# A third warm-up burst on TensorE, one store moved to ScalarE's DMA queue, and a changed place for one write and one transposing DMA

## The chip, the cores and the metric

The kernel runs on one core of a Trainium2 chip. The metric is device time in microseconds (us) for one execution. The profile is one execution of the same program; its own time is given beside its span, which runs from the first to the last instruction.

## The reference

Two independent branches start from the same normalised input, and their sum is added to the input. Sizes: 2048 tokens, width 640, hidden width 1728, all in bf16.

```python
xn = layernorm(q)                        # 2048 x 640
# branch A: long convolution over the 2048 tokens, per channel
k_shift = sum over t in 0..3 of k shifted by t tokens, times shift_k[:, t]
kv = k_shift * v
y  = irfft(rfft(kv, 4096) * rfft(ssm_k, 4096))[:2048] + kv * ssm_D
A  = xn * y
# branch B: gated feed-forward
h  = sigmoid(xn @ w_gate) * (xn @ w_up)  # 2048 x 1728
B  = h @ w_down                          # 2048 x 640
out = q + A + B
```

## The kernel before

**Tiling.** The 2048 tokens are 16 token tiles of 128 tokens (`NQ`), with the tokens on the partitions; `acc` (128 x 16 x 640) is loaded with the input, has both branches added to it and is stored from. Branch B works on four groups `tr` of four token tiles: the group is normalised (`xn`), transposed (`xnT`, width on partitions), multiplied with 14 blocks of gate and up weights (`rec_fc`, line 775; 5 matmuls of 128x512 each), passed through sigmoid (ScalarE) and multiplication (VectorE), and multiplied with `wd` (`rec_down`, line 791). Branch A is a Fourier transform in four matmul stages (lines 510, 530, 578, 610) in ten steps, written between the matmuls of branch B.

**Order.** Every piece of work is an operation with a number, given in the order in which the functions record it. The list `ORDER`, written out by hand, is the order in which the operations are issued; each engine and each DMA queue takes its own from the list in that order and goes through them strictly one after the other. `ON_DVE` names the operations that run on VectorE where both VectorE and ScalarE could do them. The keys that an operation lists as read and written (`r=`, `w=`) serve only to find out what has to stand before it in `ORDER`. The waits of the program on the chip come from the tiles that the instructions really touch.

**Queues.** Nearly all DMAs are issued by SyncE's queue, SP; four of the first loads are issued by ScalarE's. A wait of one DMA holds back everything behind it on its queue.

**The beginning.** TensorE first runs `warm`, matmuls of a zeroed tile with nothing useful in their result: 61 of 84 columns (`WARM`, operation 4). VectorE computes the statistics of token tiles 0, 1 and 2 (`rec_stat`, lines 640 and 642; `mv` is mean and variance). Tile 0's normalised rows are transposed on TensorE (operation 101, line 706, into `pst0_0`); then a second part of `warm`, 12 of 85 columns (operation 109), follows; ScalarE copies the transposed tile to `xnT` (operation 102), and the first real matmuls (operation 156, line 754) read that copy.

**Group 1, at 38 to 60 us.** Five DMAs on SP matter here. Operations 70, 71 and 73 are loads of the input for token tiles 8 to 15, each for a quarter of the partitions (32 partitions, 320 KB; line 367); the fourth quarter, 72, is issued long before. Operation 145 (line 693) writes the normalised group 1 to a scratch tensor `xnd` in DRAM. Operation 577 (line 700) reads it back as a transposing DMA into `xnT` for group 1. In the order before, SP issues 145, 73, 70, 71, 577, and behind them seven loads of the convolution's filter (line 456). The statistics of tiles 8 to 15 run on ScalarE: eight sums (`rec_stat_act`, line 647), each over all partitions of a tile and so behind all four loads. Seven of the eight stand in ScalarE's order ahead of the first sigmoid of group 1 (line 736). The matmuls of line 775 write to two PSUM slots (`g`); a gate slot is free again after its sigmoid.

**The end.** `store` writes the result: tiles 0 to 7, 8 to 13 and tile 14 each as four DMAs of 32 partitions (line 631), and tile 15 in three DMAs by column ranges 0 to 320, 320 to 560, 560 to 640 (line 627), all on SP in this order. Each waits for VectorE's last additions to its part of `acc` (lines 619 and 802).

Of the kernel before, what the change touches and what calls it, by code (L numbers as in the profile page):

```python
# [15 lines left out]
ACT = mybir.ActivationFunctionType  # L16
# [6 lines left out]
NQ = S // P  # L23
# [21 lines left out]
def _dft_tables():  # L45
# [32 lines left out]

ORDER = [
# [38 lines left out]
]  # L118
ON_DVE = [
    38, 50, 104, 108, 141, 142, 144, 148, 151, 153, 184, 186, 201, 224, 322, 415, 442, 449, 472, 486, 490, 508, 520, 811  # L120
]


# [94 lines left out]
def kernel(  # L218
# [74 lines left out]
    plan = _Plan(SLOTS, ("c", "xq"))  # L293
# [42 lines left out]
    def dma(fn, nd, run, q="SP", few=0.0, **kw):  # L336
        few = few or (1.4 if nd <= 64 and run > 1000 else 1.0)
        plan.op({q: (0.48 + nd / 8000.0, lambda: fn(nc.sync if q == "SP" else nc.scalar))},
                size=1.05 * few * nd * (10.6 + run / 23.8) / 16e3 + 0.03, nd=nd, **kw)
# [283 lines left out]
    def store(m0, m1, pri, d0=0, d1=DM):  # L623
        key = [("acc", m, x) for m in range(m0, m1) for x in range(4)] if d1 - d0 == DM else (
            [("fin", m, (d0 > 0) + (d0 > 320)) for m in range(m0, m1)] + [("cv", m) for m in range(m0, m1)])
        if m0 >= PRM["ML"]:
            dma(lambda e: e.dma_start(oq4[:, :, m0:m1, d0:d1], acc[:, m0:m1, d0:d1]), 128,
                2 * (d1 - d0) * (m1 - m0), few=3.0, r=key, w=[("out", m0, d0)], pri=pri)
            return
        for q in range(4):  # L630
            dma(lambda e, q=q: e.dma_start(oq4[q][:, m0:m1, d0:d1], acc[32 * q:32 * q + 32, m0:m1, d0:d1]), 32,
                2 * (d1 - d0) * (m1 - m0), r=key, w=[("out", m0, d0, q)], pri=pri)

    MEAN, VAR, RST, TMP, EPS = range(5)

    def rec_stat(m, pri):
        b = f"bs{m}"
        ak = [("acc", m, q) for q in range(4)]
        for s2 in range(2):
            dve(320, 1, lambda s2=s2: nc.vector.bn_stats(tl[b][:, 6 * s2:6 * s2 + 6], acc[:, m, s2 * 320:(s2 + 1) * 320]),  # L640
                r=ak, w=[(b, s2)], alloc=[(b, "bs")] if s2 == 0 else (), pri=pri)
        dve(8, 1, lambda: nc.vector.bn_aggr(st[:, 0:2, m], tl[b].rearrange("p (a c) -> p a c", a=2)),  # L642
            r=[(b, 0), (b, 1)], w=[("mv", m)], pri=pri)
# [95 lines left out]
                r=[pk(1), (sg,)], w=[(hk, fc)], pri=pri - 2000)  # L739

    MG, MD = 213.5, 135.0
    WARM = (61, 84)

    def rec_first(pri):
        every = [(fc, u) for fc in range(2) for u in range(2)]
# [62 lines left out]
    FIX = -1e6  # L808
# [9 lines left out]
    def warm(n, w=512):  # L818
        for _ in range(n):
            nc.tensor.matmul(tl["wps"][:, 0, 0:w], lhsT=tl["warm"][:, 0:P], rhs=tl["warm"][:, 0:w], start=True, stop=True)  # L820
    plan.op({"PE": (4.4, lambda: warm(*WARM))}, r=[("warm",)], w=[("wps", 0)], alloc=[("wps", "c")], pri=FIX)
    for m in range(2):
# [28 lines left out]
    rec_norm(0, FIX + 5, True)  # L851
    rec_tp(0, FIX, True)
    plan.op({"PE": (1.5, lambda: warm(12, 85))}, r=[("warm",), ("xn0", 0)], w=[("wps", 1)], pri=FIX + 0.5)
    for m0, m1, k in ((4, 8, "LS1"), (8, NQ, "LNS")):
        if m0 == 4:
            for m in range(m0, m1):
                rec_stat(m, PRM[k])
        else:
            rec_stat_act(m0, m1, PRM[k])
        rec_rsq(m0, m1, PRM[k], 1.0 if m0 == 4 else 1.0 / DM)  # L860
# [73 lines left out]
```

## Time and profile before

| | |
|---|---|
| median of 3 runs | 243.39 us (242.72, 243.39, 245.96) |
| profiled execution, own time | 242.79 us |
| profiled execution, span | 241.0 us |
| TensorE (PE) matmul busy | 230.3 us, 96% of the span |
| VectorE (DVE) busy | 198.7 us, 82% |
| ScalarE (ACT) busy | 152.2 us, 63% |
| bytes moved by DMA | 43.73 MB, 181 GB/s |

PE is TensorE's matmuls and PEld its weight loads. Rows of the timeline begin with the start and the length in us; a number in square brackets is the time for which the engine stood idle before the row, with what ended that. The suffix q (SPq, ACTq) is an engine's sequencer, which issues DMAs. In the tables by stretch, each engine's busy time is followed by the number of its instructions, then come the granted TensorE clock, the mean busy share of the 16 DMA engines, and GB/s.

### The profile page before, as it was taken

How to read it: one execution, taken by the hardware profiler on the slowest of the kernel's cores; microseconds unless marked ns; L12 is line 12 of the kernel's file. 1: busy time of each engine (PE TensorE's matmuls, PEld its weight loads, DVE VectorE, ACT ScalarE, POOL GpSimd, SP SyncE). 2: the span in 40 equal slices, each digit the busy share in tenths (PEclk: the TensorE clock that was granted, in tenths of full speed). 3: DMA queues.
4: the chain of work that ended last, by engine and by line, in shares of the span. 5: the costliest groups of instructions: out<-in, count | busy, mean ns of one | idle time of the engine just before them, and what ended most of it. 6: DMA issues, size and time to landing. Idle time of an engine off the chain costs nothing.

```text
span 241.0 us, 8367 instructions
## 1 busy us (share of the span) xinstructions
PE 230.3 (96%) x3707; PEld 142.0 (59%) x3739; DVE 198.7 (82%) x281; ACT 152.2 (63%) x213; POOL 0.7 (0%) x6
## 2 busy tenths in 40 slices
PE   7899999999999999999999999999999999999980
PEld 7755446774445556765655555777656645557670
DVE  3726884689799988999999998898978799779960
ACT  2732332086787997367998898979797742664210
POOL 1000000000000000000000000000000000000000
PEclk9999999999999999999999999999999999999998
DMA  5999999999978698994998893597361898510871
GB/s 153 314 233 311 219 291 182 236 152 147 219 177 151 102 186 214 176 280 76 157 199 201 203 213 104 113 287 175 116 177 40 214 244 280 158 61 3 215 235 46
DMA packets 92792, 43.73 MB, mean 181 GB/s; under 512 B 69780, under 2 KB 89172, under 8 KB 92500
## 3 DMA queue, kind: packets, MB, share of 16 engines
q1 hardware_dynamic: 92564, 43.04, 78.6%
q8 instruction: 29, 0.48, 0.9%
q10 hardware_dynamic: 192, 0.16, 0.2%
q14 instruction: 7, 0.06, 0.1%
HBM read 30.74 MB, written 5.24 MB: 149 GB/s over the span
## 4 chain that ended last, share of the span: by engine, by line
PE 92%; DMA 2%; issue 2%; DVE 1%; ACT 1%; DVEq 0%
PE g L775 47%; PE g L791 26%; PE c L530 9%; PE c L578 4%; PE c L510 3%; PE c L610 2%; DMA acc<-in_A_q_dram 2%; PE c L754 1%; DVE bs L640 1%; ACT st L658 0%; ACT VV L653 0%; DVE VV L684 0%; PE g L706 0%; DVE st L642 0%; DVE st L660 0%
## 5 line engine op out<-in xcount | busy, mean ns | idle before, releaser
L775 PE MATMUL g<-xnT,w 128*128 128x512 bf16 x356 | 86.5, 380 | 1.3 <-issue 0.2
L791 PE MATMUL g<-wd,hT 128*128 128x320 bf16 (+2 forms) x462 | 65.1, 295 | 0.1
L775 PEld LDWEIGHTS <-w 128*128 128x128 bf16 x380 | 35.2, 98 | 39.5 <-issue 0.6
L791 PEld LDWEIGHTS <-hT 128*128 128x128 bf16 x462 | 43.1, 98 | 16.9
L329 ACT CAST S<-c 128x1024 bf16<-128x1024 f32 (+2 forms) x41 | 39.8, 1001 | 9.5 <-PE c L530 5.3
L736 ACT ACTIVATE sig<-g 128x512 bf16<-128x512 f32 x44 | 26.4, 602 | 26.2 <-PE g L775 24.0
L738 DVE TENSOR_TENSOR hT<-sig,g 128x512 bf16<-128x512 bf16 x44 | 30.1, 685 | 15.6 <-PE g L775 14.0
L775 PE MATMUL g<-xnT,VV 128*128 128x512 bf16 x132 | 31.8, 379 | 0.5
L329 ACT CAST T<-c 128x1024 bf16<-128x1024 f32 (+1 forms) x21 | 20.7, 1010 | 9.8 <-PE c L510 6.4
L484 DVE TENSOR_TENSOR P<-kt,sT 128x2048 bf16<-128x2048 bf16 x20 | 24.2, 1220 | 0.2
L530 PEld LDWEIGHTS <-Mt 64*128 64x128 f16 x1280 | 19.8, 95 | 5.8 <-issue 5.0
L530 PE MATMUL c<-T,Mt 64*128 64x64 bf16 x1280 | 22.1, 190 | 0.5 <-issue 0.5
L775 PEld LDWEIGHTS <-VV 128*128 128x128 bf16 x140 | 13.3, 98 | 15.0
L802 DVE TENSOR_TENSOR acc<-g,acc 128x320 bf16<-128x320 f32 (+2 forms) x33 | 15.7, 479 | 7.3 <-PE g L791 6.9
L329 ACT CAST VV<-c 128x1024 bf16<-128x1024 f32 x17 | 17.0, 1020 | 4.9 <-PE c L578 4.7
L332 ACT ACTIVATE T<-c 128x1024 bf16<-128x1024 f32 x18 | 18.1, 1026 | 1.3 <-PE c L510 1.3
L647 ACT ACTIVATE VV<-acc 128x640 bf16<-128x640 bf16 x9 | 6.6, 736 | 10.8 <-DMA acc<-in_A_q_dram 10.6
L562 DVE TENSOR_TENSOR S<-S 64x2048 bf16<-64x2048 bf16 x10 | 12.2, 1220 | 0.3
L559 DVE TENSOR_TENSOR S<-S 128x2048 bf16<-128x2048 bf16 x10 | 12.2, 1224 | 0.3
L564 DVE TENSOR_TENSOR S<-P 64x2048 bf16<-64x2048 bf16 x10 | 12.2, 1223 | 0.3
L488 DVE TENSOR_TENSOR P<-P,P 128x2048 bf16<-128x2048 bf16 x10 | 12.2, 1223 | 0.2
L552 DVE TENSOR_TENSOR P<-S,P 128x2048 bf16<-128x2048 bf16 x10 | 12.2, 1220 | 0.1
(75 smaller groups left out, 181.9 us busy)
## 6 DMA issues: line engine op xcount, KB each, us to landing
P<-S SPq DMA_DIRECT2D x20, 256.0 KB, 3.9
w<-in_B_w_up_dram SPq DMA_DIRECT2D x7, 640.0 KB, 6.4
w<-in_B_w_gate_dram SPq DMA_DIRECT2D x7, 640.0 KB, 6.7
kt<-in_A_k_dram SPq DMA_DIRECT2D x8, 320.0 KB, 7.3
xnd<-VV SPq DMA_DIRECT2D x4, 640.0 KB, 5.2
vt<-in_A_v_dram SPq DMA_DIRECT2D x8, 320.0 KB, 6.8
VV<-in_A_ssm_k_dram SPq DMA_DIRECT2D x16, 96.0 KB, 4.1
wd<-in_B_w_down_dram SPq DMA_DIRECT2D x3, 480.0 KB, 8.3
```

The costliest lines, as they stand in the source:

```text
L329: fa = lambda: nc.scalar.copy(out=out_fn(), in_=in_fn())
L332: fa = lambda: nc.scalar.activation(out_fn(), in_fn(), ACT.Copy, scale=scale)
L484: dve(2048, 2, lambda: nc.vector.tensor_tensor(tl[c].rearrange("p i (n c) -> p i n c", c=CJ), two(t), sh(t), ALU.mult), r=kr + [("s",)], w ...
L488: dve(2048, 2, lambda: nc.vector.tensor_tensor(tl[a][:], tl[a][:], tl[b][:], ALU.add), r=[(b,)], w=[(a,)], pri=pri)
L530: nc.tensor.matmul(tl[c][:, b, 64 * kk:64 * kk + 64], lhsT=Mb[rows, (k + 16 * b) % 32, 64 - 64 * r:192 - 64 * r], rhs=tl[T][rows, 2 * k + ...
L552: dve(n, 2, lambda: nc.vector.tensor_tensor(Q(), X(), Q(), ALU.mult), r=[(Z, "h", 0), (Z, "h", 1)], w=[(Z, 0)], pri=pri)
L559: dve(n, 2, lambda: nc.vector.tensor_tensor(X(), X(), H(), ALU.mult), r=[(Z, 0)] + sr, w=[(S_, "p")], pri=pri + 0.01)
L736: act(512, lambda: nc.scalar.activation(tl[sg][:], pv(0), ACT.Sigmoid), r=[pk(0)], w=[(sg,)], alloc=[(sg, "sig")], pri=pri - 2000)
L738: dve(512, 1, lambda: nc.vector.tensor_tensor(hT[:, fc, :], tl[sg][:], pv(1), ALU.mult), r=[pk(1), (sg,)], w=[(hk, fc)], pri=pri - 2000)
L775: nc.tensor.matmul(tl[c][:], lhsT=w()[:, k, o:o + P], rhs=tl[X][:, k, :], start=(k == 0), stop=(k == NC - 1))
L791: nc.tensor.matmul(tl[pd[i]][:, 0:d1 - d0], lhsT=hT[:, fc, t4 * P:(t4 + 1) * P], rhs=wd[:, fc, d0:d1], start=(fc == 0), stop=(fc == NFC - 1))
L802: dve(d1 - d0, 1, lambda i=i, m=m, pd=pd, d0=d0, d1=d1: nc.vector.tensor_tensor(acc[:, m, d0:d1], tl[pd[i]][:, 0:d1 - d0], acc[:, m, d0:d1 ...
```

## The change

Three things are changed in the code, and `ORDER` and `ON_DVE` follow.

- `WARM` is 57 matmuls of 90 columns instead of 61 of 84.
- A third part of `warm`, four matmuls of 256 columns, is recorded as a new operation 110. It lists tile 1's statistics (`mv`, 1) and tile 0's transposed rows as read. It stands in `ORDER` behind operation 102 and ahead of the first real matmuls.
- In `store`, the four DMAs of tile 14 are issued by ScalarE's queue instead of SP's. Their places in `ORDER` stay.

All operations from 110 on get a number one higher, and so do the entries of `ON_DVE`. With the numbers mapped, `ORDER` differs in one more place: operation 145 (now 146, the write to `xnd`) and 577 (now 578, the transposing DMA). SP's order was 145, 73, 70, 71, 577; it is 73, 70, 146, 578, 71.

```diff
@@ ORDER
-    86, 87, 88, 15, 102, 156, 103, 104, 531, 157, 46, 47, 48, 49, 532, 68, 66, 91, 67, 92, 69, 567, 16, 158, 569, 89,
+    86, 87, 88, 15, 102, 110, 157, 103, 104, 532, 158, 46, 47, 48, 49, 533, 68, 66, 91, 67, 92, 69, 568, 16, 159, 570,
...
-    523, 524, 525, 526, 556, 590, 143, 558, 596, 142, 591, 144, 145, 594, 597, 73, 600, 598, 599, 601, 37, 38, 178,
-    586, 70, 587, 71, 577, 589, 28, 31, 30, 29, 27, 25, 26, 39, 128, 177, 124, 127, 123, 130, 129, 580, 581, 179, 578,
...
+    558, 524, 525, 526, 527, 557, 591, 144, 559, 597, 143, 592, 145, 595, 598, 73, 601, 599, 600, 602, 37, 38, 179,
+    587, 70, 146, 578, 588, 71, 590, 28, 31, 30, 29, 27, 25, 26, 39, 129, 178, 125, 128, 124, 131, 130, 581, 582, 180,
...
@@ store
         for q in range(4):
             dma(lambda e, q=q: e.dma_start(oq4[q][:, m0:m1, d0:d1], acc[32 * q:32 * q + 32, m0:m1, d0:d1]), 32,
-                2 * (d1 - d0) * (m1 - m0), r=key, w=[("out", m0, d0, q)], pri=pri)
+                2 * (d1 - d0) * (m1 - m0), q="ACT" if m0 == NQ - 2 else "SP", r=key, w=[("out", m0, d0, q)], pri=pri)
...
-    WARM = (61, 84)
+    WARM = (57, 90)
...
     plan.op({"PE": (1.5, lambda: warm(12, 85))}, r=[("warm",), ("xn0", 0)], w=[("wps", 1)], pri=FIX + 0.5)
+    plan.op({"PE": (0.43, lambda: warm(4, 256))}, r=[("warm",), ("mv", 1), ("pst0_0", 0)], w=[("wps", 2)], pri=FIX + 0.5)
```

More of the change, by code (lines that the diff above doesn't have):

```diff
@@ L80 @@
     5, 1, 6, 8, 7, 10, 9, 13, 11, 12, 20, 0, 76, 77, 78, 79, 17, 19, 80, 96, 81, 82, 83, 18, 84, 4, 85, 97, 101, 109,
[37 rows of a table removed]
[37 rows of a table added]
 ]
 ON_DVE = [
-    38, 50, 104, 108, 141, 142, 144, 148, 151, 153, 184, 186, 201, 224, 322, 415, 442, 449, 472, 486, 490, 508, 520, 811
+    38, 50, 104, 108, 142, 143, 145, 149, 152, 154, 185, 187, 202, 225, 323, 416, 443, 450, 473, 487, 491, 509, 521, 812
 ]
```

68 rows, old and new, of the table ORDER are left out of this document.

## The prediction

> **What bounds the kernel now.** First the page: the span, the slices, and the chain of work that ended last.
>
> ```profile
> span 241.0 us, 8367 instructions
> ...
> PE   7899999999999999999999999999999999999980
> ...
> PEclk9999999999999999999999999999999999999998
> ...
> PE 92%; DMA 2%; issue 2%; DVE 1%; ACT 1%; DVEq 0%
> ```
>
> TensorE is busy from the second slice to the last but one, and 92% of the chain is its work. So time that TensorE stands still anywhere in the middle stays in the total; only the first 8 us and what follows the last matmul are bounded by others. The profiled execution took 242.79 us, 1.79 outside its span; the median of the three runs, 243.39, is 0.6 above it. I sum on 242.79.
>
> The change touches three places. I read the timeline at each.
>
> **The beginning.**
>
> ```profile
> 1.22 4.45 PE L820 MATMUL c<-sig 128*128 128x84 bf16 x61 [1.22 <-DVE sig L809]
> ...
> 6.12 1.03 PE L820 MATMUL c<-sig 128*128 128x85 bf16 x12
> ...
> 6.65 0.21 DVE L642 BATCH_NORM_AGGREGATE st<-bs 128x2 f32<-128x12 f32 x1
> ...
> 7.82 0.72 PE L754 MATMUL c<-xnT,VV 128*128 128x128 bf16 x10 [0.66 <-ACT xnT L329]
> ...
> 8.82 1.30 PE L754 MATMUL c<-xnT,VV 128*128 128x128 bf16 x20
> ```
>
> The clock shows in the spacing (the page's clock row shows 9 from the start and doesn't tell these). From 12 to 61 warm-up matmuls the time grows by 3.42 us, 70 ns for each 84 columns: 0.83 ns a column. From 10 to 20 matmuls of line 754 it grows by 0.58 us, 58 ns for 128 columns: 0.45. So the clock went from half to full between 7.15 and 7.82, in the 0.66 us in which TensorE waits for ScalarE's copy.
>
> 57 x 90 is 5130 columns against 61 x 84 = 5124: the same time. The new part is 1024 columns: 0.46 us at the fast spacing, 0.85 at the slow one. It fits into the 0.66 us or ends 0.19 after them (7.15 + 0.85 = 8.00). The wait for tile 1's statistics costs nothing: they are ready at 6.65 + 0.21 = 6.86, before the second part has ended; and as the new matmuls touch neither statistics nor transposed rows, I expect no such wait in the queue at all. Queued behind it are the matmuls of line 754, which wait for the copy anyway. I take **0**, with ends -0.2 and +0.2.
>
> [...]
>
> **The middle.** This part is not in the title of the change; it is in the order list, and I think that it decides.
>
> ```profile
> 32.95 5.51 SPq L432 DMA_DIRECT2D kt<-in_A_k_dram  x2
> 40.28 0.40 SPq L693 DMA_DIRECT2D xnd<-VV  x1
> 40.72 2.10 SPq L367 DMA_DIRECT2D acc<-in_A_q_dram  x3
> 43.89 4.86 SPq L700 DMA_TRANSPOSE xnT<-xnd  x1
> 48.79 4.93 SPq L456 DMA_DIRECT2D VV<-in_A_ssm_k_dram  x7
> ```
>
> SP's order of time. From 38.5 to 40.28 SP stands before the write (its waits name VectorE's normalisation):
>
> ```profile
> SPq L693 <- DVE VV L684: 1.8, 1, 1.8
> ```
>
> The change fills that pause with two of the three loads, and puts the third behind the transposing DMA. Who waits for the third load is in ScalarE's timeline, and who waits for ScalarE in TensorE's:
>
> ```profile
> 48.62 0.74 ACT L647 ACTIVATE VV<-acc 128x640 bf16<-128x640 bf16 x1 [10.56 <-DMA acc<-in_A_q_dram]
> ...
> 54.43 0.19 ACT L647 ACTIVATION_READ_ACCUMULATOR VV<-acc 128x1 f32 x1
> 55.21 0.60 ACT L736 ACTIVATE sig<-g 128x512 bf16<-128x512 f32 x1 [0.59 <-PE g L775]
> ```
>
> ```profile
> 44.42 9.67 PE L791 MATMUL g<-wd,hT 128*128 128x320 bf16 x70
> 53.93 1.24 PE L775 MATMUL g<-xnT,VV 128*128 128x512 bf16 x4
> 55.01 3.40 PE L775 MATMUL g<-xnT,w 128*128 128x512 bf16 x15
> ```
>
> ScalarE waits 10.56 us for the last of the loads, to 48.62; seven sums take it to 54.62, and its first sigmoid of group 1 at 55.21 waited only 0.59 us for TensorE. TensorE has two PSUM slots; its second group of five runs from 55.01 to about 56.09 (3.40 us less one length of 0.38 over 14 gaps is 0.216 a matmul), and the third needs the slot which the sigmoid frees at 55.81. So a load later by more than 0.59 + 0.28, about 0.8 us, stops TensorE for the excess.
>
> How late is it? In time on the DMA engines:
>
> ```profile
> 38.50:39.50 1.00, 1.00 (x9) 0.66 (x7) 0.69 (x2) 0.00 (x0) 0.00 (x0) 1.00 0.43 40
> ...
> 40.28:43.81 3.53, 3.53 (x28) 2.54 (x27) 0.98 (x2) 0.00 (x0) 0.00 (x0) 1.00 1.13 309
> 43.81:48.60 4.79, 4.79 (x37) 3.49 (x36) 4.01 (x6) 0.00 (x0) 0.00 (x0) 1.00 1.01 189
> ```
>
> The DMA share (last but one) is full from 40.28 on. The write lands 3.5 us after its issue (the least of line 693), and the transposing DMA lands 9.1 after its own (the least of line 700):
>
> ```profile
> DMA to landing us min/median/max: 3.5/5.2/6.5
> ```
>
> ```profile
> DMA to landing us min/median/max: 9.1/9.3/9.5
> ```
>
> So: write landed 43.8; three loads landed 48.6, 4.8 us later, 1.6 each; transposing DMA landed 43.89 + 9.1 = 53.0, 4.4 after the loads, 0.9 ahead of the matmuls that read it at 53.93.
>
> After the change, step by step:
> 1. Two loads are in the queue ahead of the write: its landing moves by 2 x 1.6 to **47.0** (46.0 if the hole at 38.5 takes some of them; 43.8 if all).
> 2. SP waits there; the transposing DMA is issued at 47.1. Another one in the trace blocked SP for 2.79 us:
>
> ```profile
> 97.31 2.79 SPq L700 DMA_TRANSPOSE xnT<-xnd  x1
> ```
>
> SP is free at 49.9. The third load is issued by 50.4.
> 3. With nothing ahead of it the transposing DMA lands between 47.1 + 4.4 = 51.5 and 47.1 + 9.1 = 56.2. In before, 4.7 of the 9.1 went by beside the loads, so the nearer row is the 4.4; with half a microsecond to start, 52.0. TensorE needs it at 53.93: no stall.
> 4. The third load is behind it in the same queue. At 1.0 us after, it lands at **53.0**, 4.4 later than 48.6. Less the 0.8 of slack, TensorE stops for **3.6 us** at about 56 to 60. Bounds: 0 (write not delayed: 43.89 + 2.79, then an issue and a short landing, about 49.4) and +7.8 (transposing DMA at 56.2, load at 57.2).
>
> The seven filter loads move back by 1.6 us (48.79 to 50.4). Their first use on TensorE is here, and moves by 3.6, which hides it:
>
> ```profile
> 60.50 0.41 PE L510 MATMUL c<-Ft,VV 32*128 32x64 f16 x32
> ```
>
> **The end.**
>
> ```profile
> 232.75 0.82 DVE L619 TENSOR_TENSOR acc<-acc,vt 128x1280 bf16<-128x1280 bf16 x1
> 233.67 0.49 DVE L802 TENSOR_TENSOR acc<-g,acc 128x320 bf16<-128x320 f32 x1
> 234.87 0.74 DVE L802 TENSOR_TENSOR acc<-g,acc 128x240 bf16<-128x240 f32 x2 [0.71 <-PE g L791]
> ```
>
> ```profile
> 233.60 1.71 SPq L631 DMA_DIRECT2D out_dram<-acc  x4
> 235.40 1.95 SPq L627 DMA_DIRECT2D out_dram<-acc  x3
> ```
>
> ```profile
> SPq L929 <- DMA out_dram<-acc: 2.1, 1, 2.1
> ```
>
> Tile 14's four issues hold SP until 235.31. Tile 15's first part was ready at 234.16, its last at 234.87 + 0.74 = 235.61. The three issues take 1.95 us, 0.65 each, the last from 236.7; then 2.1 us of landing. With the four on the other queue: first part 234.2 to 234.85, second (ready about 235.25) to 235.9, third to 236.55 instead of 237.35. ScalarE is idle there (its last row is a 0.69 us copy at 230.52) and has issued loads beside SP at no higher price:
>
> ```profile
> 0.73 1.84 ACTq L367 DMA_DIRECT2D acc<-in_A_q_dram  x4
> ```
>
> I take **-0.9**; nothing (0) if the stores share what limits the landing, -1.2 if the first part's start sets it.
>
> **Sum:** 242.79 + 0 + 3.6 - 0.9 = **245.5**.
>
> **The rivals.**
> *The load is not late (not slower).* If the two early loads go through in the hole of 38.5 to 39.5 (share 0.43) and in the 1.8 us for which SP stood, the write lands near 43.8, the third load near 49.4, and the middle costs nothing: 242.79 - 0.9 = 241.9. It decides where the third load lands before 49.4. For it: the pause is real. Against it: the two loads of `k` ahead on SP (32.95 + 5.51) end their issue only at 38.46, so data of theirs are still to come, and the share is 1.13 right after. Chance 0.2.
>
> *The clock falls in the new pause.* TensorE would stand for over 3 us. At the end of the kernel the clock record holds after the last matmul and has fallen later:
>
> ```profile
> 235.40:238.90 3.50, 0.00 (x0) 0.00 (x0) 0.21 (x1) 0.00 (x0) 0.00 (x0) 1.00 0.26 67
> 238.90:241.00 2.10, 0.00 (x0) 0.00 (x0) 0.00 (x0) 0.00 (x0) 0.00 (x0) 0.55 0.02 4
> ```
>
> So 3.5 us idle did not lower it, a little more did. If it falls, TensorE runs at half speed until it is raised; at the beginning that took at most 7.82 - 1.22 = 6.6 us, so up to 3.3 us are lost: 245.5 + about 3 = 248.5. Chance 0.1. [...]
>
> *The transposing DMA is slow on an empty queue too.* Landing toward 56.2 and the load behind it: 247.5 to 249.7. Chance 0.1.
>
> *The change doesn't do what it says:* no wait for the statistics exists in the queue. The time is the same 245.5, so it has no share of its own.
>
> **How the numbers follow.** Forecast 0.6 (243.5 to 247.0: write landing 46 to 47.5, load 0.5 to 1.6 behind the transposing DMA, end -0.4 to -1.2). The range goes from the first rival, 241.9, to the beginning of the two slow ones, 248.4. A measurement tells 2% from no change, 4.9 us here: 238.5 and 248.3. Nothing gives the former, 0.02; about two thirds of the slow rivals pass the latter, 0.14; the rest, 0.84, is within.
>
> **What would show it.** The new burst between 7.0 and 7.9 with line 754 still at about 7.8. SP's row of line 700 near 47 instead of 43.89, and a single load of line 367 behind it. ScalarE's line 647 starting near 53 instead of 48.62, idle for it about 15 us, and an idle gap of 3 to 4 us on TensorE before a group of line 775 at 59 to 60, with the sigmoid's row no longer waiting for TensorE. At the end, four stores on ACTq and the row of line 627 beginning at 234.2. I am wrong if line 647 starts before 49.5, if the pause is made up later, or if the granted clock dips behind it.

## The result and the profile after

The changed kernel took **251.6 us** (median of 6 runs, 249.5 to 252.8) against 243.61 us for the kernel before beside it (6 runs, 242.72 to 245.96): a ratio of 1.0309, 95% interval 1.0266 to 1.0353. It is 3% slower. The forecast was 245.5 us with a range of 241.9 to 248.4; the time lies outside it.

The profiled execution took 251.6 us, with a span of 249.8 against 241.0: 8.8 us to explain. First the page of the changed kernel: the span, the slices, the clock and the chain that ended last.

```profile
span 249.8 us, 8367 instructions
...
PE   8889999992999999999999999999999999999990
...
PEclk9999999998699999999999999999999999999998
...
PE 68%; DMA 13%; SPq 8%; ACT 6%; issue 2%; DVE 1%; DVEq 0%; ACTq 0%
```

Two things are new. In the tenth slice TensorE is busy for two tenths, and in the tenth and eleventh the granted clock is 0.8 and 0.6. The chain, 92% TensorE before, now goes for a quarter through DMA, SP and ScalarE. The number of instructions is the same. Apart from the third slice (8, before 9), the rest of these rows looks like before, so most of the loss should lie around 56 to 68 us.

**The middle.** SP's order of time, and its longest wait there:

```profile
40.32 1.89 SPq L367 DMA_DIRECT2D acc<-in_A_q_dram  x2
42.33 0.40 SPq L693 DMA_DIRECT2D xnd<-VV  x1
48.43 2.76 SPq L700 DMA_TRANSPOSE xnT<-xnd  x1
51.25 0.56 SPq L367 DMA_DIRECT2D acc<-in_A_q_dram  x1
51.87 4.20 SPq L456 DMA_DIRECT2D VV<-in_A_ssm_k_dram  x7
```

```profile
SPq L700 <- DMA xnd<-VV: 5.6, 1, 5.6
```

SP stands 5.6 us before the transposing DMA, until the write to `xnd` has landed; the third load comes behind. Then ScalarE and TensorE:

```profile
55.48 0.74 ACT L647 ACTIVATE VV<-acc 128x640 bf16<-128x640 bf16 x1 [16.63 <-DMA VV<-in_A_ssm_k_dram]
...
61.37 1.06 ACT L736 ACTIVATE sig<-g 128x512 bf16<-128x512 f32 x2
```

```profile
55.27 1.24 PE L775 MATMUL g<-xnT,VV 128*128 128x512 bf16 x4
56.35 1.24 PE L775 MATMUL g<-xnT,w 128*128 128x512 bf16 x5
62.00 4.42 PE L775 MATMUL g<-xnT,w 128*128 128x512 bf16 x10 [4.41 <-ACT sig L736]
```

ScalarE's first sum starts at 55.48 instead of 48.62, after 16.63 us of waiting for a DMA. (The row names a load of the filter: the releaser is inferred, and the sum reads `acc`, and nothing that the filter's load writes. By the trace's record of its semaphore, the third load landed at 55.45.) Seven sums later the two sigmoids run back to back at 61.37, no longer waiting for TensorE. TensorE stood for 4.41 us, up to 62.00.

Then a second loss: ten matmuls of 512 columns take 4.42 us, where the same ten took 2.32 elsewhere in this trace. The table by stretch shows the granted clock (the column behind POOL):

```profile
57.60:60.25 2.65, 0.00 (x0) 0.00 (x0) 0.63 (x1) 2.56 (x7) 0.00 (x0) 1.00 0.90 150
...
60.30:61.95 1.65, 0.00 (x0) 0.00 (x0) 0.00 (x0) 1.62 (x6) 0.00 (x0) 0.50 1.39 175
62.00:67.05 5.05, 5.05 (x12) 1.72 (x12) 2.56 (x4) 1.95 (x6) 0.00 (x0) 0.50 1.40 184
67.15:69.00 1.85, 1.85 (x20) 0.72 (x21) 1.05 (x2) 0.72 (x2) 0.00 (x0) 1.00 0.57 236
```

The clock fell 2.7 us into the pause and was at half until 67.1. TensorE worked through 5.1 us of that at half speed, and so lost about 2.5.

**The beginning.**

```profile
1.22 4.45 PE L820 MATMUL c<-sig 128*128 128x90 bf16 x57 [1.22 <-DVE sig L809]
...
5.99 1.06 PE L820 MATMUL c<-sig 128*128 128x85 bf16 x16
7.85 0.72 PE L754 MATMUL c<-xnT,VV 128*128 128x128 bf16 x10 [0.81 <-ACT xnT L329]
```

The third part of the warm-up follows the second at once; the row counts both, 12 and 4. Its 2044 columns took 1.06 us, the 1020 of before 1.03: in this execution the clock was already up. Nothing waits for tile 1's statistics. Line 754 starts at 7.85, against 7.82 before.

**The end.** The stores, and SP's wait ahead of line 627:

```profile
241.99 2.24 ACTq L631 DMA_DIRECT2D out_dram<-acc  x4
...
244.72 1.95 SPq L627 DMA_DIRECT2D out_dram<-acc  x3
```

```profile
SPq L627 <- DMA out_dram<-acc: 2.9, 1, 2.9
```

In the kernel before, the same wait was:

```profile
SPq L627 <- DVE acc L802: 0.3, 1, 0.3
```

Tile 14's stores are on ScalarE's queue, yet SP's row of line 627 doesn't begin earlier against the work that it follows, but later: 0.99 us behind the last matmul's end, which was 0.07 before. SP waited there 0.3 us for VectorE; now it waits 2.9 for a DMA that stores. The span ends 6.10 us behind the last matmul instead of 5.67.

**Together:** 4.4 (stop) + 2.5 (half clock) + 0.4 (end) = 7.3 of the 8.8 us. Another 1.3 is there before the middle begins (the first group of line 775 starts at 55.27 instead of 53.93), where TensorE waits for loads of weights:

```profile
PE g L775 <- DMA VV<-in_B_w_up_dram: 0.6, 1, 0.6
PE g L791 <- DMA wd<-in_B_w_down_dram: 0.4, 1, 0.4
```

The next experiments show the same groups at 54.23 to 55.07 in kernels with SP's order of before, so I don't count this part as the change's.

### The profile page after: what moved, and what is told of

The parts are those of the page before. It is cut to its first block, busy times and chain, and to the rows that moved or that the text cites. A ratio compares the mean times of both kernels' runs of the same rounds, so it can differ in the third digit from the quotient of the medians.

```text
span 249.8 us, 8367 instructions
## 1 busy us (share of the span) xinstructions
PE 233.3 (93%) x3707; PEld 142.4 (57%) x3739; DVE 198.7 (80%) x281; ACT 151.9 (61%) x213; POOL 0.7 (0%) x6
## 4 chain that ended last, share of the span: by engine, by line
PE 68%; DMA 13%; SPq 8%; ACT 6%; issue 2%; DVE 1%; DVEq 0%; ACTq 0%
PE g L775 32%; PE g L791 21%; PE c L530 7%; DMA acc<-in_A_q_dram 4%; PE c L578 4%; DMA wd<-in_B_w_down_dram 3%; SPq L367 3%; PE c L510 3%; SPq L421 2%; DMA P<-S 2%; PE c L610 2%; ACT VV L647 2%; DMA VV<-in_B_w_gate_dram 2%; DMA VV<-in_A_ssm_k_dram 1%; ACT VV L653 1%
## 5 line engine op out<-in xcount | busy, mean ns | idle before, releaser
L775 PE MATMUL g<-xnT,w 128*128 128x512 bf16 x356 | 88.8, 386 | 5.7 <-ACT sig L736 4.4
L775 PEld LDWEIGHTS <-w 128*128 128x128 bf16 x380 | 35.7, 99 | 45.3 <-issue 7.2
L775 PE MATMUL g<-xnT,VV 128*128 128x512 bf16 x132 | 32.4, 383 | 1.1 <-DMA VV<-in_B_w_up_dram 0.6
L775 PEld LDWEIGHTS <-VV 128*128 128x128 bf16 x140 | 13.4, 99 | 16.5 <-issue 1.1
L329 ACT CAST VV<-c 128x1024 bf16<-128x1024 f32 x17 | 17.0, 1020 | 4.9 <-PE c L578 4.7
```

Source lines behind the costliest of these rows:

```text
L329: fa = lambda: nc.scalar.copy(out=out_fn(), in_=in_fn())
L775: nc.tensor.matmul(tl[c][:], lhsT=w()[:, k, o:o + P], rhs=tl[X][:, k, :], start=(k == 0), stop=(k == NC - 1))
```

## The experiments

My theory after the traces: the changed place of 145 and 577 on SP makes almost all of the loss, by two steps, a stop behind the late third load and a clock that falls in the stop; the end costs a little, because tile 15's stores wait for tile 14's. The rivals: warm-up or stores take part in it; the late write and the late transposing DMA cost the time wherever the third load stands; the clock falls for a reason other than the pause; the two queues' stores slow each other.

A list of `ORDER` of another length moves the line numbers by two in e1, e2 and e4 (L777 for L775), and added lines move them by four to six in e8 to e13. "Behind the last matmul" is counted from the end of TensorE's last row.

### One part at a time: e1 to e4

e1 is the kernel before with only the changed order on SP:

```diff
-    ..., 144, 145, 594, 597, 73, ..., 586, 70, 587, 71, 577, 589, 28, ...
+    ..., 144, 594, 597, 73, ..., 586, 70, 145, 577, 587, 71, 589, 28, ...
```

> The kernel before with one thing changed: SP's order 73, 70, 145, 577, 71. Theory A (the late load is the loss): TensorE stops 4.6 us ahead of line 775 near 60 us, the clock falls to half for 5 to 7 us, and nothing else is lost: 243.6 + 4.6 + 2.5 = 250.7, 249.5 to 251.5. Rival B (the order costs only the stop of 3.6 that I predicted, the rest comes from the warm-up or the end): 247. Rival C (the loss of 1.3 us between 16 and 40 us in the changed kernel's profile also belongs to the order): 252.

e2 is the changed kernel with the order put back, e3 has only the four stores of tile 14 on ScalarE's queue, e4 only the warm-up (`WARM`, the third part, and its place).

> The changed kernel with SP's order put back to 145, 73, 70, 71, 577. Theory A: line 647 starts near 48.6 again, no stop and no fall of the clock; what is left is the end: 243.6 to 244.6. Rival B: 246 to 248. My prediction's term for the end: 242.7.

> The kernel before with tile 14's four stores on ScalarE's queue, nothing else. Theory D (the three stores of tile 15 wait for semaphores that the four stores of tile 14 have just taken): the row of line 627 begins about 2.7 us after the first of the four, at 236.3 instead of 235.40, and the time is 0.4 to 0.9 longer: 244.1 to 244.5. Prediction: the row begins at 234.2 and 0.9 is saved, 242.7.

> The kernel before with the warm-up in three parts, stores and order as before. Theory and prediction: no change, 243.4 to 243.8, the first matmuls of line 754 still at 7.8. Rival E (the 1.3 us lost between 16 and 40 us come from the beginning): 244.9, with TensorE waiting for a weight load near 16 us in the profile.

| | median us | ratio to before (243.13), 95% interval |
|---|---|---|
| e1, order alone | 250.1 (246.4 to 251.2, 4 runs) | 1.0221 (1.0146 to 1.0295) |
| e2, all but the order | 243.87 | 1.0012 (0.9984 to 1.0040) |
| e3, stores alone | 243.43 | 1.0025 (0.9996 to 1.0054) |
| e4, warm-up alone | 243.74 | 1.0024 (0.9999 to 1.0050) |

e1's ratio is worked out from its executions of 246.4 and 249.9 us alone; its median is 1.029 times that of the kernel before. The clearer comparison is the changed kernel (1.0309) with e2 (1.0012), which differ in nothing but the order; in e2 the sums begin at 49.79, and TensorE doesn't stop there. So the order alone makes the loss, and the two edits that give the change its name make none that 2% would show. e1's timeline of TensorE and its clock by stretch:

```profile
62.29 4.42 PE L777 MATMUL g<-xnT,w 128*128 128x512 bf16 x10 [4.98 <-ACT sig L738]
```

```profile
62.30:67.60 5.30, 5.30 (x13) 1.86 (x13) 2.55 (x4) 2.20 (x6) 0.00 (x0) 0.50 1.28 244
```

Stop and half clock are both there. One of e1's four executions, the one of 246.4 us, kept its clock (mean 0.997, the others 0.985 to 0.989); the others took 3.5 to 4.8 us more. How long TensorE stopped in it isn't known, as it was not profiled. All six executions of the changed kernel have means of 0.981 to 0.989.

e4's profile has the beginning of the changed kernel (line 754, here L756, at 7.72 behind a gap of 0.59) and an end like before. In e3 SP's stores of tile 15 begin 0.97 us behind the last matmul, with the same kind of wait as in the changed kernel:

```profile
237.70 1.95 SPq L627 DMA_DIRECT2D out_dram<-acc  x3
```

```profile
SPq L627 <- DMA out_dram<-acc: 3.5, 1, 3.5
```

e3's span ends 6.09 us behind the last matmul, as late as the changed kernel's. e3 and e4 also had short stops of about 1 us at 57 to 58, behind sums that began at 51.50 and 50.98; the order of before leaves the loads that little room, and its stop comes and goes with the execution.

### The place of the third load: e5

```diff
-    ..., 144, 145, 594, 597, 73, ..., 586, 70, 587, 71, 577, 589, 28, ...
+    ..., 144, 594, 597, 73, ..., 586, 70, 587, 71, 145, 577, 589, 28, ...
```

> The kernel before with all three input loads ahead of the write on SP: 73, 70, 71, 145, 577. It separates the place of the third load from the later write. Theory (the third load behind the transposing DMA holds ScalarE's sums, and they hold the first sigmoids): the sums start at 47 to 49; the write lands some 1.6 us later than in the changed kernel (48.4), near 50, the transposing DMA 4.9 after it, near 54.9, against a need at 53.9: TensorE stops for 0 to 1.2 us, its clock holds, and the time is 243.1 to 244.5 us. Rival (it is the late write and the late transposing DMA that cost the time, wherever the third load stands): 248 to 251 us, as with the changed order.

245.01 us; ratio 1.0071 (1.0040 to 1.0102) against 243.63 beside it. SP, and what TensorE waited for from 5 to 60 us:

```profile
41.05 2.35 SPq L367 DMA_DIRECT2D acc<-in_A_q_dram  x3
43.51 0.40 SPq L693 DMA_DIRECT2D xnd<-VV  x1
50.88 2.79 SPq L700 DMA_TRANSPOSE xnT<-xnd  x1
```

```profile
PE g L791 <- DMA wd<-in_B_w_down_dram: 1.4, 1, 1.4
...
PE g L775 <- DMA xnT<-xnd: 0.2, 1, 0.2
```

The transposing DMA is issued later than in the changed kernel (50.88 against 48.43), and costs 0.2 us of waiting. The sums begin at 49.54, and the clock holds: ten matmuls of 512 columns take 2.32 us at 60.18. So neither the late write nor the late transposing DMA makes the loss; the third load behind them does. The median is 0.5 us above the range I gave, and 1.4 above the kernel before. The profiled execution (246.59 us) lost 1.4 us to the loads of `wd` at 40 us; whether the others did isn't known.

### The sums behind the sigmoids: e7

SP's order is the changed one; ScalarE's eight sums are moved, each behind a sigmoid, and with them their mean (131) and three of the squares that need it.

```diff
-    ..., 39, 128, 177, 124, 127, 123, 130, 129, ..., 126, ..., 621, 638, 125, 131, ..., 654, ..., 617, ..., 171, ..., 657, ..., 629, ..., 633, ...
+    ..., 39, 177, ..., 621, 128, 638, 124, ..., 654, 127, ..., 617, 123, ..., 171, 130, ..., 657, 129, ..., 629, 126, ..., 633, 125, 131, ...
```

> The kernel before with SP's changed order, and with ScalarE's eight sums of tiles 8 to 15 moved behind the first eight sigmoids of group 1, one behind each, and the squares that follow them moved on accordingly. It separates the order on ScalarE from the order on SP. Theory (the late load costs only because the sums stand ahead of the sigmoids in ScalarE's order): the first sums wait no more than the load's landing at 55 to 56, the first sigmoid is not behind them, TensorE does not stop at 56 to 62 beyond about 1 us, the clock holds, and the time is 242.5 to 244.5 us. Rival (the late transposing DMA, or the filter's loads behind the third load, cost it): 246 us or more with the stop still there.

245.88 us; ratio 1.0072 (1.0043 to 1.0102). TensorE's timeline:

```profile
55.26 3.40 PE L775 MATMUL g<-xnT,w 128*128 128x512 bf16 x15
...
77.10 1.24 PE L775 MATMUL g<-xnT,VV 128*128 128x512 bf16 x5 [0.95 <-ACT hT L329]
```

The load is as late as in the changed kernel (SP issues it at 51.3), and TensorE goes through 55 to 62 us without a stop, at full speed (fifteen matmuls in 3.40 us). The stop thus needs both orders: the load late on SP, and the sums ahead of the sigmoids on ScalarE. The time is 1.4 us above what I gave: the moved sums now delay other work of ScalarE and VectorE, with waits of 0.2 to 1.0 us at 66 to 77 us (the last row is one). The rival's 246 us is near in time, but its stop isn't there.

### The clock: e6 and e9

Both have the changed order and 20 matmuls without use in the stop. e9 takes 20 matmuls out of the first warm-up burst, with as many columns.

```diff
-    ..., 638, 125, 131, 637, 42, ...
+    ..., 638, 125, 131, 883, 637, 42, ...
+    def keep(n, w):
+        for _ in range(n):
+            nc.tensor.matmul(tl["keep"][:, 0, 0:w], lhsT=tl["w0_4"][:, 0, 0:P], rhs=wd[:, 0, 0:w], start=True, stop=True)
+    plan.op({"PE": (4.0, lambda: keep(20, 512))}, ...)
```

```diff
-    WARM = (61, 84)
+    WARM = (41, 125)
```

> The kernel before with SP's changed order, and with 20 matmuls of 512 columns without use on TensorE in the stop (4.3 us of work at 0.216 us each, ahead of the third group of line 775). It separates the stop from the fall of the clock. Theory (the clock falls because TensorE has nothing to do for 4 to 5 us): the granted clock holds through 56 to 68 us, the sigmoid still waits for the late load, and the time is that of before plus the stop alone, 243.1 + 3.5 to 4.6 = 246.6 to 247.7 us. Rival (the clock falls for another reason in this order, for instance DMA load): the clock is 0.5 for some 7 us all the same, and the time is 249.5 to 251 us. If the matmuls themselves take the place of the stop and lengthen it, the third group starts when they end and not behind the sigmoid.

> As e6 (the kernel before, SP's changed order, 20 matmuls of 512 columns in the stop), but the first warm-up burst has 20 matmuls fewer and as many columns (41 of 125 instead of 61 of 84), so that behind the stop TensorE's program stands where it stood in the kernel before. In e6 the clock held, but two gaps of 1.8 and 1.5 us, behind which the profile shows no releaser, stood at 174 and 222 us, where no other kernel here has any. Theory (these gaps come from the place of the instructions, as 20 more move all behind them, and are no part of the change): the gaps are gone, the clock holds through 56 to 68 us, the third group of line 775 starts at 61 to 62.5, and the time is before plus the stop, 243.5 + 3.3 to 5.6 = 246.8 to 249.1 us, some 2 to 4 under e6. Rival (the gaps belong to the changed order of the DMAs, and are part of its cost): they stand there again, 250.5 to 252 us. Should the clock fall all the same, then the pause isn't its cause.

e6: 251.84 us, ratio 1.0311 (1.0262 to 1.0360). The clock held (1.00 from 56.00 to 60.40 and from 60.50 to 68.00), and the time was still that of the fall. TensorE's waits from 60 us on show why:

```profile
PE c L610 <- issue: 1.8, 2, 1.5
PE c L578 <- issue: 1.8, 1, 1.8
```

Two gaps of 1.5 and 1.8 us, far behind the edit, for which the profile names no releaser ("issue"). The kernel before has 0.6 and 0.5 there. They are most of the 4.6 us between e6 and e9 below; the rest wasn't traced. Had I stopped at e6, its time would have said that the clock costs nothing.

e9: **247.26 us** (247.21 to 247.76), ratio 1.0169 (1.0123 to 1.0214) against 243.3. TensorE, its clock by stretch, and its waits from 60 us on:

```profile
54.96 1.24 PE L775 MATMUL g<-xnT,w 128*128 128x512 bf16 x5
56.04 4.48 PE L905 MATMUL c<-wd,w 128*128 128x512 bf16 x20
61.29 2.32 PE L775 MATMUL g<-xnT,w 128*128 128x512 bf16 x10 [0.77 <-ACT sig L736]
```

```profile
60.50:68.00 7.50, 6.68 (x62) 3.04 (x62) 4.88 (x7) 5.68 (x14) 0.00 (x0) 1.00 1.18 190
```

```profile
PE g L775 <- ACT sig L736: 0.8, 1, 0.8
PE c L530 <- issue: 0.2, 1, 0.2
PE g L775 <- issue: 0.2, 1, 0.2
```

The two gaps are gone, so they came with the 20 added matmuls, as the theory said; why the place of the instructions makes a gap is not shown. The third group still waits for the sigmoid, to 61.29: from its earliest start, 56.04, that is a stop of 5.25 us with the matmuls in it. The clock held all through (1.00 in the row of 60.50 to 68.00, and from 56.00 to 60.40). So the pause is the fall's cause, and the loss has its two sizes: the stop alone costs 4.0 us in the median (247.26 against 243.3), stop and fall 7.0 (e1, 250.1 against 243.13), and the fall by difference **3.0 us**, from four executions each.

### The end: e8 and e10 to e14

By the semaphores' records in the traces of before and of the changed kernel, the program's DMAs on SP and ScalarE take eight completion semaphores in turn, and in all 153 pairs of each trace a DMA is issued only after the one before it on its semaphore has landed. In the changed kernel tile 14's four stores take four of them, those of tiles 8 to 13 the other four, and tile 15's three the first three again: tile 14's. The first of tile 14's lands at 244.66 us, and SP issues tile 15's first, on the same semaphore, at 244.72. In the kernel before they fell on those of tiles 8 to 13, which had landed at 233.04 to 234.86, ahead of the issues from 235.40 on. The new turn also puts the stores of tiles 8 to 13 on semaphores of a late load and of tiles 0 to 7: the last of them is issued 2.9 us ahead of the last matmul's end, 4.8 before. To take the sharing away, the number of DMAs has to be changed.

```diff
 e8: tile 14 as one DMA of 128 partitions on ScalarE's queue
 e10: no store of tile 14
 e11: tile 14 as two DMAs of 64 partitions on ScalarE's queue
 e12: tile 14 as in the change; tiles 8 to 13 as one DMA of 128 partitions
 e13: tile 14 as in the change; no store of tiles 8 to 13
 e14: tile 15 as four DMAs of 32 partitions, in place of three by columns:
-    store(15, 16, 247.0, d1=320)
-    store(15, 16, 248.0, d0=320, d1=560)
-    store(15, 16, 249.0, d0=560)
+    store(15, 16, 247.0)
```

> The kernel before with tile 14's result stored by ScalarE's queue, as in the change, but as one DMA of 128 partitions instead of four of 32. The eight completion semaphores which all DMAs take in turn then give tile 15's three stores others than tile 14's. Theory (tile 15's stores wait because they share semaphores with tile 14's): the first of tile 15's three issues begins about 1.1 us ahead of the end of the last matmul, where it began 0.06 behind it in the kernel before and 0.97 behind it with tile 14's four stores on ScalarE's queue; the end lies 4.8 us behind the last matmul instead of 5.67 and 6.09; the time is 0.8 us under the kernel before, 242.3 us. Rival (the stores of both queues share the DMA engines, so that it is the transfers that delay each other): the row begins early but the end stays 5.7 to 6.1 us behind the last matmul, and the time is 243.1 to 243.5 us.

> The kernel before without the store of token tile 14, which leaves that part of the output unwritten; it is a bound on what freeing SP's queue at the end can bring. Theory A (the issue on SP bounds the end, as the prediction's -0.9 has it): tile 15's first store is issued 1.1 us ahead of the last matmul's end instead of 0.06 behind it, and the span ends 4.8 us behind the last matmul instead of 5.67; 242.7 us. Theory B (tile 15's own data, ready 0.3 us behind the last matmul, and their landing bound it): the first is issued early, but the end stays 5.4 to 5.7 us behind the last matmul; 243.2 to 243.6 us. In e8 the issues were 0.8 earlier and the end 0.1 later, with a single slower DMA for tile 14 beside them: by A that was tile 14's DMA in the way.

> The kernel before with tile 14's result stored by ScalarE's queue as two DMAs of 64 partitions, between the change's four of 32 and e8's one of 128. Tile 15's first two stores then share no completion semaphore with tile 14's, and the third shares one with the first of the two. Theory (shared semaphores made tile 15's issues late in the change, and the transfers beside them made the landing late in e8): the first issue is 1.1 us ahead of the last matmul's end, the landing lies between those of e8 and of the kernel before, and the end 5.2 to 5.7 us behind the last matmul; 243.0 to 243.6 us. Rival (any store on ScalarE's queue delays SP's): the first issue 0.5 or more behind the last matmul's end, as in the change (1.0), the end 6.1 behind it, 244 us.

> The kernel before with tile 14's four stores of 32 partitions on ScalarE's queue, exactly as in the change, and with the result of tiles 8 to 13 stored by SP as one DMA of 128 partitions instead of four of 32. No DMA of the last eleven but three then remains to share a semaphore: tile 15's three stores take semaphores that neither tile 14's nor tiles 8 to 13's use. Theory (in the change, tile 15's stores were late by the shared semaphores alone, and the four on ScalarE's queue would otherwise be as good as none on SP): the first of tile 15's issues stands 1.1 us ahead of the last matmul's end, the end 4.2 to 4.8 us behind it (4.19 without tile 14's store, 5.67 in the kernel before, 6.09 in the change), and the time is 0.5 to 1.2 us under the kernel before, 242.1 to 242.8 us. Rival 1 (any store beside SP's on the other queue slows the landing, as in e8 and e11): the issues are early, the end 5.7 to 7.8 us behind the last matmul, 243.3 to 245.5 us. Rival 2 (the one DMA for tiles 8 to 13 lands late, as tile 14's did as one DMA): its landing, not tile 15's, is the last, with the same 243.3 to 245.5 us.

> The kernel before with tile 14's four stores of 32 partitions on ScalarE's queue, as in the change, and without the store of tiles 8 to 13, which leaves that part of the output unwritten. Tile 15's three stores then share no completion semaphore with tile 14's, and no DMA of another form stands beside them, as it did in e8, e11 and e12. Theory (the late issues in the change come from the shared semaphores, and those four stores on ScalarE's queue do not slow the landing): the first of tile 15's issues stands 1.1 us ahead of the last matmul's end, the end 4.2 to 4.8 us behind it, and the time is 0.8 to 1.4 us under the kernel before, about 242.4 us if that gives 243.5. Rival (stores on two queues slow each other's landing in any form): issues early, the end 5.4 us or more behind the last matmul, 243.3 us or more.

> The kernel before with tile 15's result stored as four DMAs of 32 partitions over all 640 columns, issued by SP behind tile 14's, instead of three DMAs of 128 partitions by column ranges; nothing else is changed. It tests whether the form of tile 15's stores bounds the landing (all DMAs of 128 partitions here had few DMA engines busy: a share of 0.23 to 0.31 of the sixteen, and tiles 8 to 13 as one took 16 us), and it may beat both kernels. Theory (the form bounds it): the first issue stands 0.3 us behind the last matmul's end, the fourth ends 2.1 behind it, the data land 1.2 us later, and the end lies 4.6 us behind the last matmul instead of 5.67: 1.0 us under the kernel before, about 242.5 us if that gives 243.5. Rival (what follows the landing bounds the end, or the later start of the first part costs what the form gains): 5.4 us or more behind the last matmul, 243.2 us or more.

| | tile 15's first issue, us behind the last matmul | end of span, us behind it | ratio to before, 95% interval |
|---|---|---|---|
| before | 0.07 | 5.67 | |
| e3 (four on ScalarE's queue) | 0.97 | 6.09 | 1.0025 (0.9996 to 1.0054) |
| e8 | -1.14 | 5.77 | 1.0042 (1.0011 to 1.0074) |
| e10 | -1.14 | 4.20 | 0.9956 (0.9924 to 0.9987) |
| e11 | -1.14 | 7.83 | 1.0089 (1.0061 to 1.0118) |
| e12 (profiled execution 256.25 us) | -1.14 | 14.72 | 1.0368 (1.0333 to 1.0403) |
| e13 | -1.14 | 4.39 | 0.9964 (0.9936 to 0.9992) |
| e14 | 0.31 | 4.69 | 0.9972 (0.9949 to 0.9995) |

The times are 244.76, 242.19, 245.46, 252.91, 242.73 and 243.26 us for e8 and e10 to e14. Wherever nothing is shared, the first issue goes out 1.14 us ahead of the last matmul's end, as the prediction had it. e11 has both cases side by side, since only its third store of tile 15 shares a semaphore with tile 14: SP's waits there, at line 627 of before (L633 here),

```profile
SPq L633 <- DVE acc L808: 3.3, 2, 2.6
...
SPq L633 <- DMA out_dram<-acc: 2.5, 1, 2.5
```

are for VectorE twice, and for a store once. e13, with the change's own four stores, has no such wait and no other slow DMA, and ends 4.39 us behind the last matmul. Its rival, that stores on two queues slow each other in any form, asked for 5.4 or more and fails. So the prediction's term was right as far as the issue goes; the shared semaphores made it 0.4 the other way. e13 also has no transfers of tiles 8 to 13 beside these stores, so its end is a bound and not the size of the sharing.

e8, e11 and e12 issue as early, and end late. What they have in common is a large DMA of 64 or 128 partitions. e12 with TensorE and all others done:

```profile
242.80:245.90 3.10, 0.00 (x0) 0.00 (x0) 0.00 (x0) 0.00 (x0) 0.00 (x0) 0.50 0.31 114
...
249.10:251.00 1.90, 0.00 (x0) 0.00 (x0) 0.00 (x0) 0.00 (x0) 0.00 (x0) 0.50 0.13 33
```

The mean DMA share is 0.31 and 0.13 in these stretches, with data waiting, and the one store of tiles 8 to 13 landed some 16 us after its issue. Beside it tile 14's four of 32 partitions, 40 KB each, took 7.5 us from issue to landing; in the changed kernel they took 1.7, beside four stores of tiles 8 to 13 that took 3.8 (medians). In the kernel before, by the semaphores' records, tile 15's three stores of 128 partitions (20 to 80 KB) took 2.8 to 3.1 us, tile 14's four of 32 partitions 1.6 to 2.0. So rival 2 of e12's expectation holds in that the one store lands late, and for e8 and e11 the same cause is likely. Why a store of many partitions is so slow was not shown.

e14 uses the quicker form: tile 15 as four DMAs of 32 partitions ends 4.69 us behind the last matmul, although its first issue is later. It is the one kernel with the whole output that is faster than both, by 0.28% (0.05 to 0.51), some 0.7 us, against the kernel before; its theory gave 1.0.

## Why the prediction was wrong, point by point

**Beginning, 0: right.** Line 754 at 7.85 (7.82 before); no wait for the statistics exists in the queue, as expected; e4 gives 1.0024 (0.9999 to 1.0050). The burst ended at 7.05, within the gap that was there. As the clock was already up, the slow price of 0.85 us and the end at +0.2 were not put to the test. (In the kernel before it rose at 6.99 us by its record, a little ahead of the 7.15 that I read.)

**Middle, +3.6: mechanism right, size too small.** All its marks came: line 700 late, one load behind it, the sums late, the sigmoid not waiting for TensorE; and so did one sign of being wrong, the clock that dips behind the pause. By step:
1. SP stood until 48.4 for the write instead of 47.0. 1.3 of that is the later start of this execution: in e9, which had none, line 700 was issued at 46.91. Right.
2. SP was free of the transposing DMA 2.76 us later (2.79 forecast). Right.
3. The transposing DMA landed without stopping TensorE, by its semaphore 4.8 us after its issue (48.43 to 53.24; 4.9 forecast; 6.2 in e9). Right.
4. **This failed in size:** "at 1.0 us after" was a guess without a row. The third load landed 2.2 us after the transposing DMA (55.45), 2.0 in e1 and 1.6 in e9. So the sums could begin 4.2 us after SP began to issue it (51.25 to 55.48; 5.0 in e9, 49.71 to 54.76), where my steps left 3.1. What made it that long wasn't traced. The stop became 4.4 us here, 5.0 in e1 and 5.25 in e9. In the median it cost 4.0 (e9); the kernel before has gaps of 0.5 and 0.6 us at 173 and 230 us that e9's profile lacks.

**The clock, 0.1: the step that failed most.** I had this rival with the right mechanism and price (up to 3.3 us; e9 against e1: 3.0; in the trace 2.5), but with a tenth of the chance. The step behind it was "3.5 us idle did not lower it, a little more did". That took one pause for a threshold. Other ends show that it is none; e10's, where the last matmul ended at 235.40:

```profile
235.45:237.55 2.10, 0.00 (x0) 0.00 (x0) 0.23 (x1) 0.00 (x0) 0.00 (x0) 1.00 0.24 68
237.65:238.50 0.85, 0.00 (x0) 0.00 (x0) 0.00 (x0) 0.00 (x0) 0.00 (x0) 0.50 0.10 17
```

Here the clock fell 2.2 us after the last matmul; at the end of before 3.8 after it, in the changed kernel's stop 2.7 and at its end 4.3, in e11 about 4.5 (an estimate from its mean clock of 0.68 between 238.30 and 240.90; its last matmul ended at 234.75). So the length of the pause alone doesn't tell, and what does was not shown. Two of these five falls came within the 3.6 us of the stop that I forecast, so a tenth was too little; with the stops that came, of 4.4 and 5.0 us, the fall was the likely case, and holding the clock was the rare one (by the mean clocks, one execution of the ten of e1 and the changed kernel). The stop of 1.0 us in e3 brought no fall: the ten matmuls behind it took 2.32 us.

**End, -0.9: wrong in sign, +0.4.** The four issues left SP, ScalarE was idle, and tile 15's data were ready, all as said. The step that failed is that SP would be free: I read the queue and not what its DMAs wait for. Of the bounds (0 to -1.2) neither allowed for a cost. (The rows of the working give 0.8, from 237.35 to 236.55, and not 0.9.) Without the shared semaphores it would have been -1.3 to -1.5 at most (ends of 4.39 in e13 and 4.20 in e10 against 5.67), as both leave out a store. The +0.4 is read from the profiles; in the times of e2 and e3 it is within the noise, but their intervals rule out a saving of 0.9.

**Sum.** By what the runs gave: 242.79 + 0 + 4.4 + 2.5 + 0.4 + 1.3 (the late weights in this execution) = 251.4, against 251.6 measured. The stop's size alone would have stayed within the range (e9: 247.26); the clock put it outside. The rival's own 248.5 was short too: by 0.8 for the stop, 1.3 for the end and 1.3 for the late weights, less 0.5 for the fall.

**Other rivals.** *The load is not late:* no, the pause of 1.8 us on SP was not enough. *The transposing DMA is slow:* no, it landed at 53.24 and TensorE didn't wait for it; in e5, where it was issued at 50.88, 0.2 us. *No wait for the statistics:* true, and without effect.

## What to carry to other kernels

Where an in-order engine has a job that nothing urgent needs (the sums) ahead of one that TensorE needs (the sigmoids), the job's input becomes urgent (here TensorE stopped for 4.4 us); moving a load on a DMA queue has to be followed to the last engine that takes its work in order. A stop of TensorE as long as these, 4.4 to 5.0 us, should be priced with half-speed time behind it as the likely case: here 3.0 us behind a stop that cost 4.0. Moving DMAs to an idle queue frees the issuer only if nothing left behind waits for them: tile 15's first store, on a completion semaphore of tile 14's, waited 2.9 us. And a store's shape counts: tiles 8 to 13 landed within 6.4 us as four DMAs and took some 16 as one.

## What the runs showed of the hardware that was not expected

- The clock's fall in a pause came 2.2 to 4.5 us after the last matmul, at no fixed length (above). It also hit the beginning: in e8, whose beginning is that of the kernel before, the first burst took 3.99 us instead of 4.45, so the clock rose before its end; TensorE then waited 0.55 us and, after 0.9 us of work, 1.46 us, until 8.14. The granted clock is 1.00 from 5.80 to 7.90, 0.50 from 8.00 to 11.30 and 1.00 from 11.40 on. TensorE did 3.2 us of work at half speed, so about 1.6 were lost. Whether the third part of the warm-up guards against this was not tried.
- Twenty more matmuls at 56 us brought gaps of 1.8 and 1.5 us at 174 and 222 us (e6), which twenty fewer at the start took away (e9).
- The same 983 kB of tiles 8 to 13 landed within 6.4 us of their first issue as four DMAs (before), and some 16 us after their issue as one (e12).
